# Attention on one Trainium2 core: the last 64 keys scored by one fp32 product in 64x64 tiles at the head of each pair, two GpSimd additions in every pair, and another order of score and maxima units

## Chip, core and metric

One core of one Trainium2 chip runs the kernel. The metric is device time in microseconds (us), the median of repeated runs. Engines are named as the profile names them: PE (TensorE, matrix products), PEld (its weight loads), DVE (VectorE), ACT (ScalarE), POOL (GpSimd), SP (the engine that issues most DMAs).

## What is computed

Attention over 4 batches and 8 heads (576 positions, 64 values per head), then two feed-forward layers on its output. Only the attention changes here:

```python
q_rot, k_rot = (rotate(q), rotate(k))
scores = scale * np.matmul(q_rot, k_rot.transpose(0, 1, 3, 2))
scores = scores - np.max(scores, axis=-1, keepdims=True)
attn = np.exp(scores)
attn = attn / (np.sum(attn, axis=-1, keepdims=True) + 1e-09)
return np.matmul(attn, v).astype(np.float32)
```

Everything is float32 with a tight tolerance. A score product is therefore made of three products of rounded parts (high by high, low by high, high by low, each in the type fp32r), or of one product in full fp32.

## The kernel before

**Pairs.** The work is tiled in 16 pairs of heads (`NPAIR`), one after the other. A pair's two heads lie in partitions 0 to 63 and 64 to 127. The feed-forward layers follow the 16 pairs and are not touched.

**What a pair's phase does.** `phase(i)` interleaves two kinds of unit on PE, each into one of four PSUM slots `PS[0]` to `PS[3]` (two banks each):

- score units of pair i, `st_unit`: letter `t` in the order string, eight per pair, 128 keys by 288 queries. Each has four products for each of the two heads (L663): three of rounded parts, and one that subtracts the row maxima (`one_r` by `mr`). The two heads use the upper and lower half of the array at once (tile form 64x128). ACT then takes the exponential into a tile `E`. Letter `T` is the ninth unit, for the last 64 keys: eight products of the form 128x128 (L671), whose weights `KRH` and `KRL` are block-diagonal copies of the last keys, made by DMAs.
- maxima units of pair i+1, `s_unit`: its own scores in one rounded product, from which DVE takes row maxima. Letter `x` (two per pair) covers two query chunks by 256 keys, `y` (four) one chunk by 320 keys (both L611), `S` the last 64 queries (L621, form 128x128). `s_end` combines the maxima, and three small DMAs lay them out as the row tile `MR` of the next pair.

The order is a string that is written out by hand, `"ytyttxtttyttyxTS"`. `phase` gives each unit a slot by a small model of when slots come free: among the free ones the latest freed, else the one that is free first. The last four units use only slots 0 to 2.

**After the phase**, still in pair i: eight groups of fp32 products of `E` with the values into `PS[3]` (L700, tiles 128x32), the row sums by products with ones (L735, `sum_unit`), and the values of the last 64 keys (L710, tiles 64x64, four at once). ACT and DVE copy `PS[3]` out as `xu`. `add_unit` lets POOL add some `E` tiles beforehand into `AC`, so that the row sums need fewer products: two additions for pairs before `FOUR` (9) and for the last, four for pairs 9 to 14. Two additions leave four groups of four products in `sum_unit`, four additions three.

**Beside it** DVE rotates q and k of pair i+2 in the tile `RAW` (`prep_high`, two buffers), ACT casts the high parts `QP`, `QH`, `KH`; POOL subtracts for the low part `QL`, and for `KL` up to pair 9; from then on `KL` is DVE's. `prep_load` loads `RAW` of pair i+2. In the earlier pairs DVE also converts weights of the next layer (`wa_half`).

**Order.** A planner (`Plan`) lists the tasks of each engine by modelled times; PE's tasks keep the order in which the code adds them.

Of the kernel before, what the change touches and what calls it, by code (L numbers as in the profile page):

```python
# [23 lines left out]
FOUR = 9  # L24
# [146 lines left out]
def mixer_kernel(ctx: ExitStack, tc: tile.TileContext, qk, v, vrem, cs, w_in, g_ln, w_sgT, b_sg,  # L171
# [58 lines left out]
    KRH = tiles(att, "krh", 3, [128, 128], F32R)  # L230
    KRL = tiles(att, "krl", 3, [128, 128], F32R)
    MR = tiles(att, "mr", 2, [128, S], F32R)
    MX = tiles(att, "mx", 2, [128, 2, 2, 4], F32)
    MN = tiles(att, "mn", 2, [128, 10], F32R)
    VM = tiles(att, "vm", 2, [128, 4, 2, 64], F32)
    VR = tiles(att, "vr", 2, [128, 64], F32)
# [8 lines left out]
    one_r = att.tile([128, 128], F32R, name="one_r")  # L245
    one_b = att.tile([128, 128], F32R, name="one_b")
# [29 lines left out]
    def setup():  # L276
        def zeros(k):
            for t in (QR[k], KRH[k], KRL[k]):
                nc.gpsimd.memset(t.bitcast(F32), 0.0)
        def consts():  # L280
            nc.gpsimd.memset(one_r.bitcast(F32), 0.0)
            nc.gpsimd.memset(one_b.bitcast(F32), 0.0)
            for h in range(2):
                nc.gpsimd.memset(ones_b[h], 0.0)
            nc.gpsimd.memset(ones, 1.0)
            nc.gpsimd.memset(mhalf, -0.5)
            for t in (*XS, *RB):
# [163 lines left out]

    def dg(q, dst, src):
        for h in range(2):
            q.dma_start(out=dst[64 * h:64 * h + 64, 64 * h:64 * h + 64].bitcast(F32),
                        in_=src[64 * h:64 * h + 64, 512:576].bitcast(F32))
    def first_pairs():
# [29 lines left out]
        def cast_qp(i, x, y, n):  # L486
            acopy(lambda: QP[i][:, :, x // 4:y // 4], lambda: RAW[i][:, 0, 0, x:y].rearrange("r (p c) -> r c p", c=4), n,
                  [("raw", i, 0, 0), ("raw", i, 0, 1)][x // HALF:1 + (y > HALF)], [("qpx" if y < 512 else "qp", i)])

        def low(i, j, r=()):  # L490
# [3 lines left out]
            if j:  # L494
                dma(32, lambda q: dg(q, KRL[i], KL[i]), [("kl", i)], [("krl", i)], n=2)

        def diagonals(i, j):
            hi, to, kh, kt = ((QH, QR, "qh", "qr"), (KH, KRH, "kh", "krh"))[j]
            dma(32, lambda q: dg(q, to[i], hi[i]), [(kh, i)], [(kt, i)], n=2)
# [14 lines left out]
        cast_qp(0, 0, 512, 1100)  # L514
# [4 lines left out]
        diagonals(0, 0)  # L519
        diagonals(0, 1)  # L520
# [17 lines left out]
        cast_qp(1, 0, 512, 1100)  # L538
# [4 lines left out]
        diagonals(1, 0)  # L543
        diagonals(1, 1)
# [14 lines left out]
    def prep_high(i, after):  # L559

        j2, j3 = i % 2, i % 3
        for j in (0, 1):
            raw, kr = RAW[j2][:, j], ("raw", j2, j)
            tt("D", lambda raw=raw: raw, lambda raw=raw: raw, lambda: cst, ALU.mult, 2 * S, [("cst",)], [kr], after)
            after = [tt("D", lambda raw=raw: raw[:, 0], lambda raw=raw: raw[:, 0], lambda raw=raw: raw[:, 1], ALU.add, S, [], [kr])]
            if j:
                acopy(lambda: KH[j3], lambda raw=raw: raw[:, 0], S, [kr], [("kh", j3)])
                dma(32, lambda q: dg(q, KRH[j3], KH[j3]), [("kh", j3)], [("krh", j3)], n=2)
            else:
                acopy(lambda: QP[j2], lambda raw=raw: raw[:, 0, 0:512].rearrange("r (p c) -> r c p", c=4), 1100, [kr], [("qp", j2)])  # L570
# [4 lines left out]
    def low_part(e, i, j, after):  # L575
# [5 lines left out]
        if j:  # L581
            dma(32, lambda q: dg(q, KRL[j3], KL[j3]), [("kl", j3)], [("krl", j3)], n=2)
# [7 lines left out]
    def load_v(i, after=()):  # L590
        j2 = i % 2

        def ld(q):
            q.dma_start(out=VM[j2].rearrange("p c h d -> p (c h d)"), in_=v[i // HP, i % HP])
            q.dma_start(out=VR[j2], in_=vrem[i // HP, i % HP])
        dma(290, ld, w=[("vm", j2), ("vr", j2)], after=after, n=2)

    def s_unit(i, n, ps, kps):
# [3 lines left out]
        if n < 6:  # L602
# [10 lines left out]
            add("PE", MAXIMA[n // 2 > 0][0], mm, [("qp", j2), ("kh", j3) if i > 1 or n > 1 else ("khx", i), *[("qpx", i)][:i == 0]], [kps])  # L613
# [12 lines left out]
    def s_end(i):  # L626
# [21 lines left out]
    ne = [0]  # L648
    EU = {}

    def st_unit(i, u, ps, kps):
# [3 lines left out]
        if u < 8:  # L655
# [3 lines left out]
            def mm():  # L659
                for o, (x, y) in enumerate(((kh, qh), (kl, qh), (kh, ql), (one_r, mr))):  # L660
                    for h in range(2):
                        rows = slice(64 * h, 64 * h + 64)
                        nc.tensor.matmul(ps[:, h, 0:HALF], x[rows, keys] if o < 3 else x[rows], y[rows, cols],  # L663
                                         start=o == 0, stop=o == 3)
            add("PE", 4 * PASS, mm, [("qh", j3), ("ql", j3), ("kh", j3), ("kl", j3), *[("mr", j2, x) for x in range(2 + hf)], ("consts",)], [kps])
        else:
            def mm():
                for hf in range(2):
                    cols = slice(HALF * hf, HALF * hf + HALF)
                    for o, (x, y) in enumerate(((KRH[j3], qh), (KRL[j3], qh), (KRH[j3], ql), (one_b, mr))):  # L670
                        nc.tensor.matmul(ps[:, hf, 0:HALF], x, y[:, cols], start=o == 0, stop=o == 3)  # L671
            add("PE", 8 * PASS + 0.2, mm, [("krh", j3), ("krl", j3), ("qh", j3), ("ql", j3), *[("mr", j2, x) for x in range(3)], ("consts",)], [kps])
        n = ne[0] % 9
        ne[0] += 1
        EU[i, u] = n
# [14 lines left out]
    def pv_unit(i, us):  # L690
# [15 lines left out]
        def mm():  # L706
            for hf in range(2):
                for h in range(2):
                    rows = slice(64 * h, 64 * h + 64)
                    nc.tensor.matmul(pv[64 * hf:64 * hf + 64, h, 0:HALF], VR[j2][rows], e[rows, hf], start=False, stop=True,  # L710
                                     skip_group_check=True)
        add("PE", FP32 + 0.1, mm, [("e", EU[i, 8]), ("vr", j2)], [kp])
# [4 lines left out]
        def st(q):  # L717
            for hf in range(2):
                q.dma_start(out=xu_d[i // HP][i % HP, :, HALF * hf:HALF * hf + HALF].rearrange("(h d) c -> d h c", h=2),
                            in_=xu[64 * hf:64 * hf + 64])  # L720
        dma(290, st, [("xu", j2, h) for h in range(2)], [("xu_d", i)], n=2)

    def sum_unit(i, ps, kps):

        j2 = i % 2
        src = [(ones, ones, [(E[EU[i, u + hf]], h) for h in range(2) for hf in range(2)], ("e", EU[i, u]),
# [517 lines left out]
```

## Time and profile before

| | |
|---|---|
| median of 3 runs | 552.18 us (551.42 to 552.51) |
| the profiled execution, own time | 550.86 us |
| its span | 549.1 us |
| PE busy | 541.2 us (99%) |
| DVE, ACT, POOL busy | 76%, 51%, 45% |
| granted PE clock | 0.999 of full speed |

The span runs from the first to the last instruction that the profile holds; the execution's own time is 1.8 us longer. Products on PE overlap: a product's row begins when its weights load or its first column goes in, and the time from one row's start to the next tells the pace, not the row's length. The columns of each view are said with its first group below.

### The profile page before, as it was taken

To read this page: it belongs to the slowest core of one execution; us is meant where nothing else is said; L and a number is where in the kernel's file an instruction comes from. 1 tells how busy PE (TensorE), PEld (TensorE's weight loads), DVE (VectorE), ACT (ScalarE), POOL (GpSimd) and SP (SyncE) were. 2 spreads that over 40 slices of the span, in tenths; PEclk is the share of its full clock that TensorE was granted. 3 is DMA by queue.
4 is the path that set the end of the run, shared out by engine and by line. 5 is a ranking of instruction groups with operands and counts; after the bars stand their busy time and mean duration, and the time that the engine had idled before them with its cause. 6 is when DMAs were issued, how large, how long until landed. Compare 5 with 4: busy or idle time off the path is not lost.

```text
span 549.1 us, 12848 instructions
## 1 busy us (share of the span) xinstructions
PE 541.2 (99%) x5104; PEld 462.5 (84%) x5104; DVE 416.6 (76%) x611; ACT 278.4 (51%) x451; POOL 245.7 (45%) x229
## 2 busy tenths in 40 slices
PE   7999999999999999999999999999999999999996
PEld 6877777777777777679989989989999998899985
DVE  7878888888888888878478845663989997659610
ACT  3566767667766667635527136135156443333221
POOL 6545555555555555446886776653610011222000
PEclk9999999999999999999999999999999999999999
DMA  5565656565556673773384752634264212110022
GB/s 193 136 186 154 194 143 189 150 178 175 168 164 161 185 205 95 216 240 93 133 280 134 223 198 74 210 113 144 106 214 130 66 45 78 38 58 1 0 78 96
DMA packets 58028, 77.46 MB, mean 141 GB/s; under 512 B 29392, under 2 KB 34000, under 8 KB 57968
## 3 DMA queue, kind: packets, MB, share of 16 engines
q1 hardware_dynamic: 57664, 76.37, 45.8%
q8 instruction: 40, 0.66, 0.5%
q10 hardware_dynamic: 304, 0.26, 0.1%
q14 instruction: 20, 0.16, 0.1%
HBM read 55.94 MB, written 18.95 MB: 136 GB/s over the span
## 4 chain that ended last, share of the span: by engine, by line
PE 97%; DVE 1%; POOL 0%; ACT 0%; issue 0%; ACTq 0%; POOLq 0%
PE psa L843 55%; PE psa L663 13%; PE psa L700 12%; PE psa L735 5%; PE psa L611 4%; PE psa L671 4%; PE psa L710 2%; PE psa L954 2%; PE psa L756 1%; DVE mx L614 1%; PE psa L621 1%; DVE raw L260 0%; DVE mn L623 0%; POOL mr L295 0%; ACT ob L264 0%
## 5 line engine op out<-in xcount | busy, mean ns | idle before, releaser
L614 DVE TENSOR_REDUCE mx<-psa 128x2 f32<-128x640 f32 (+1 forms) x96 | 88.7, 954 | 21.9 <-PE psa L611 14.6
L676 ACT ACTIVATE e<-psa 128x576 f32<-128x576 f32 x144 | 88.1, 652 | 20.9 <-PE psa L671 10.3
L700 PE MATMUL psa<-e,vm 128*32 128x288 f32 x1024 | 65.4, 408 | 0.0
L700 PEld LDWEIGHTS psa<-e,vm 128*32 128x32 f32 x1024 | 31.6, 110 | 27.8 <-issue 2.6
L261 POOL TENSOR_TENSOR ac<-e,e 128x576 f32<-128x576 f32 x32 | 45.0, 1425 | 8.2 <-ACT e L676 8.2
L843 PE MATMUL psa<-s_h,vn 128*128 128x288 f32 x256 | 46.9, 295 | 0.0
L260 DVE TENSOR_TENSOR raw<-raw,cst 128x1152 f32<-128x1152 f32 (+1 forms) x33 | 41.9, 1271 | 0.3 <-DMA raw<-qk 0.3
L264 ACT CAST qp<-raw 128x512 fp32r<-128x512 f32 x16 | 19.1, 1192 | 43.6 <-DVE raw L260 43.6
L663 PE MATMUL psa<-qh,kh 64*128 64x288 f32 x256 | 39.6, 305 | 0.0
L843 PEld LDWEIGHTS psa<-s_h,vn 128*128 128x128 f32 x256 | 38.3, 188 | 0.0
L663 PE MATMUL psa<-qh,kl 64*128 64x288 f32 x256 | 37.9, 292 | 0.0
L663 PE MATMUL psa<-ql,kh 64*128 64x288 f32 x256 | 37.9, 292 | 0.0
L663 PE MATMUL psa<-mr,one_r 64*128 64x288 f32 x256 | 37.7, 290 | 0.0
L261 POOL TENSOR_TENSOR vs<-vs,u 128x576 f32<-128x576 f32 x16 | 26.7, 1666 | 20.7 <-DVE vs L958 20.7
L611 PE MATMUL psa<-kh,qp 64*128 64x320 f32 (+1 forms) x256 | 32.8, 312 | 0.7 <-ACT kh L264 0.7
L1035 DVE SCALAR_TENSOR_TENSOR gt<-xm,cw,gt 128x576 f32<-128x576 f32 x32 | 28.9, 909 | 1.8 <-ACT gt L1032 1.4
L611 PEld LDWEIGHTS psa<-kh,qp 64*128 64x128 f32 x256 | 21.6, 184 | 8.0 <-ACT ss L739 3.9
L843 PE MATMUL psa<-XL,w_h 128*128 128x288 f32 x128 | 27.4, 296 | 0.0
L843 PE MATMUL psa<-XH,w_h 128*128 128x288 f32 x128 | 27.4, 295 | 0.0
L843 PE MATMUL psa<-XH,w_l 128*128 128x288 f32 x128 | 27.4, 295 | 0.0
L843 PE MATMUL psa<-s_l,vn 128*128 128x288 f32 x128 | 27.2, 294 | 0.0
L261 POOL TENSOR_TENSOR xl<-xs,xh 128x576 fp32r<-128x576 f32 x2 | 4.6, 2322 | 48.8 <-ACT xh L264 48.8
(182 smaller groups left out, 1488.2 us busy)
## 6 DMA issues: line engine op xcount, KB each, us to landing
raw<-qk SPq DMA_DIRECT2D x31, 576.0 KB
xu_d<-xu SPq DMA_DIRECT2D x32, 144.0 KB
rb<-r_d SPq DMA_DIRECT2D x32, 144.0 KB
xs<-xu_d SPq DMA_DIRECT2D x16, 288.0 KB
x_d<-xs SPq DMA_DIRECT2D x16, 288.0 KB
g_d<-vs SPq DMA_DIRECT2D x16, 288.0 KB
vm<-v SPq DMA_DIRECT2D x16, 256.0 KB
wr<-w_in SPq DMA_DIRECT2D x8, 512.0 KB
```

The costliest lines, as they stand in the source:

```text
L260: return add("DVE", dve(n), lambda: nc.vector.tensor_tensor(out_(), a(), b(), op), r, w, after, lock=True)
L261: return add("Pool", pool(n), lambda: nc.gpsimd.tensor_tensor(out_(), a(), b(), op), r, w, after, lock=True)
L264: return add("Act", act(n), lambda: nc.scalar.copy(out_(), in_()), r, w, after)
L611: nc.tensor.matmul(ps[:, h, w * y:w * y + w], QP[j2][rows, c], kh[rows, keys], start=True, stop=True)
L614: add("DVE", MAXIMA[n // 2 > 0][1], lambda: nc.vector.tensor_reduce(out=MX[j2][:, n // 2 > 0, :, chunks[0]:chunks[-1] + 1], in_=ps[:, :, 0 ...
L663: nc.tensor.matmul(ps[:, h, 0:HALF], x[rows, keys] if o < 3 else x[rows], y[rows, cols], start=o == 0, stop=o == 3)
L671: nc.tensor.matmul(ps[:, hf, 0:HALF], x, y[:, cols], start=o == 0, stop=o == 3)
L676: add("Act", 0.62, lambda: nc.scalar.activation(E[n], ps[:, :, 0:HALF], AF.Exp), [kps], [("e", n)])
L700: nc.tensor.matmul(pv[32 * t:32 * t + 32, h, 0:HALF], VM[j2][:, j, h, 32 * (t % 2):32 * (t % 2) + 32], E[EU[i, us[t // 2]]][:, h], start=j ...
L735: nc.tensor.matmul(ps[32 * t:32 * t + 32, 0, 0:HALF], x[t // 2], a[:, y], start=n == 0, stop=n == len(src) - 1, skip_group_check=True)
L843: nc.tensor.matmul(out_(y), lhs(p, k, y), rhs(q, k, y), start=not z, stop=ends and z == len(terms) - 1)
L1035: add("DVE", dve(S) + 0.05, lambda dd=dd, m=m, x2=x2, gt=gt: nc.vector.scalar_tensor_tensor(gt(), x2()[:, m:m + S], cw[:, 5 * dd + m:5 * d ...
```

## The change

- **Last 64 keys.** `t_unit(i)` stands at the head of pair i, right behind the last product of pair i-1: four fp32 products (64 keys by 288 queries; two heads by two query halves) on the rotated `RAW` tile itself, into `PS[0]`. Unit `T` is then only the two products that subtract the maxima. `KRH`, `KRL`, `one_b` and the DMAs that filled them are gone.
- **Maxima row.** `MR` is folded to 288 columns (four rows in place of two), with one `one_r` for each query half. Every score unit now waits for all three of its DMAs.
- **Order.** `T` comes first, `S` into the middle of the phase (or, in pair 0, one unit before the end), an `x` near the end.
- **Additions.** `FOUR` is 15: two POOL additions in all pairs, and `KL` by POOL in all pairs.
- **Smaller things.** k's rotation sum and its cast are cut at column 256 (one more DVE and one more ACT instruction per pair). The values of the last keys come with the others in one DMA, `xu` leaves in one. `RAW` of pair i+2 is loaded behind `t_unit(i)`, since that now reads the same buffer. At the start 29 products of 288 columns keep PE going in place of 16 of 512.

```diff
-FOUR = 9
+FOUR = 15
+FREE3 = 1.2
+ORDERS = 'xtyTtyttyytxttSt', 'TytytxttStyyttxt', 'Ttttttttt'
...
+    def t_unit(i):
+
+        raw = RAW[i % 2]
+
+        def mm():
+            for hf in range(2):
+                for h in range(2):
+                    rows = slice(64 * h, 64 * h + 64)
+                    nc.tensor.matmul(PS[0][64 * hf:64 * hf + 64, h, 0:HALF], raw[rows, 1, 0, 512:S], raw[rows, 0, 0, HALF * hf:HALF * hf + HALF],
+                                     start=True, stop=False, skip_group_check=True)
+        add("PE", FP32 + 0.1, mm, [("raw", i % 2, j) for j in range(2)], [("ps", 0)])
...
         else:
             def mm():
-                for hf in range(2):
-                    cols = slice(HALF * hf, HALF * hf + HALF)
-                    for o, (x, y) in enumerate(((KRH[j3], qh), (KRL[j3], qh), (KRH[j3], ql), (one_b, mr))):
-                        nc.tensor.matmul(ps[:, hf, 0:HALF], x, y[:, cols], start=o == 0, stop=o == 3)
...
+                for h in range(2):
+                    rows = slice(64 * h, 64 * h + 64)
+                    nc.tensor.matmul(ps[:, h, 0:HALF], one_r[2][rows], mr[rows], start=False, stop=True, skip_group_check=True)
...
-            order = "ytyttxtttyttyxTS" if i + 1 < NPAIR else "ttttttttT"
-            if not i:
-                order = "xtttyttytyttyxTS"
-            free = [0.0, 0.0, 0.74 if i else 0.0, 0.0]
-            pe, ac, dv = 0.2, 0.0, 0.0
+            order = ORDERS[1 if i + 1 < NPAIR else 2] if i else ORDERS[0]
+            free = [9.9, 0.0, 0.5 if i else 0.0, FREE3]
+            pe, ac, dv = 0.58, 0.85, 0.0
...
+                k = 0 if what == "T" else max(at_once, key=lambda k: free[k]) if at_once else min(ks, key=lambda k: free[k])
...
         for i in range(NPAIR):
+            t_unit(i)
             if i + 2 < NPAIR:
                 prep_load(i + 2)
```

**Place one, PE at the head of a pair** (`kh`, `qp`: operands of the maxima units; `mr` with `one_r`: the maxima row). Before:

```order
L735 MATMUL psa<-e_166,ones_b_181 32x288 x2
L710 MATMUL psa<-e_166,vr_156 64x288 x4
L611 MATMUL psa<-kh_133,qp_137 128x320 x2
L663 MATMUL psa<-qh_126,kh_132 128x288 x2
L663 MATMUL psa<-qh_126,kl_135 128x288 x2
```

Now:

```order
L717 MATMUL psa<-e_158,vm_149 64x288 x4
L657 MATMUL psa<-raw_123 64x288 x4
L680 MATMUL psa<-mr_142,one_r_171 128x288 x2
L610 MATMUL psa<-kh_131,qp_138 128x320 x2
L673 MATMUL psa<-qh_127,kh_133 128x288 x2
```

Four fp32 products of the form 64x64 and two of the form 64x128 have come in between the last values product and the first maxima unit.

**Place two, PE at the end of a phase before**, where the two units of the form 128x128 stand side by side:

```order
L611 MATMUL psa<-kh_133,qp_137 128x256 x4
L671 MATMUL psa<-qh_126,krh_143 128x288
L671 MATMUL psa<-qh_126,krl_146 128x288
L671 MATMUL psa<-ql_129,krh_143 128x288
L671 MATMUL psa<-mr_149,one_b 128x288
L621 MATMUL psa<-kh_133,qr_141 128x288 x2
L700 MATMUL psa<-e_158,vm_155 32x288 x2
```

And now, where `S` (L620) is the only one left and stands between two score units:

```order
L673 MATMUL psa<-ql_130,kh_133 128x288 x2
L673 MATMUL psa<-mr_142,one_r_170 128x288 x2
L620 MATMUL psa<-kh_131,qr_139 128x288 x2
L673 MATMUL psa<-qh_127,kh_133 128x288 x2
L673 MATMUL psa<-qh_127,kl_136 128x288 x2
```

The eight products of the old ninth unit are gone, and the 128x128 form is entered and left in mid-phase.

## Rows read from the trace of the kernel before

**Rows 1.** The page, part 1: busy us (share of the span) xinstructions.

```profile
PE 541.2 (99%) x5104; PEld 462.5 (84%) x5104; DVE 416.6 (76%) x611; ACT 278.4 (51%) x451; POOL 245.7 (45%) x229
```

**Rows 2.** The page, part 4: the chain that ended last, by engine and line.

```profile
PE 97%; DVE 1%; POOL 0%; ACT 0%; issue 0%; ACTq 0%; POOLq 0%
PE psa L843 55%; PE psa L663 13%; PE psa L700 12%; PE psa L735 5%; PE psa L611 4%; PE psa L671 4%; PE psa L710 2%; PE psa L954 2%; PE psa L756 1%; DVE mx L614 1%; PE psa L621 1%; DVE raw L260 0%; DVE mn L623 0%; POOL mr L295 0%; ACT ob L264 0%
```

**Rows 3.** PE timeline, one pair: start us, us, engine, line, operation, out<-in, tile, xcount.

```profile
101.14 0.41 PE L611 MATMUL psa<-kh,qp 64*128 64x320 f32 x2
101.39 0.29 PE L663 MATMUL psa<-qh,kh 64*128 64x288 f32 x2
...
102.58 0.40 PE L663 MATMUL psa<-qh,kh 64*128 64x288 f32 x2
102.81 0.29 PE L663 MATMUL psa<-qh,kl 64*128 64x288 f32 x2
...
106.32 0.55 PE L611 MATMUL psa<-kh,qp 64*128 64x320 f32 x6
106.80 0.40 PE L671 MATMUL psa<-qh,krh 128*128 128x288 f32 x1
107.03 0.30 PE L671 MATMUL psa<-qh,krl 128*128 128x288 f32 x1
...
107.97 0.42 PE L621 MATMUL psa<-kh,qr 128*128 128x288 f32 x2
108.32 4.09 PE L700 MATMUL psa<-e,vm 128*32 128x288 f32 x64
```

**Rows 4.** PE timeline in the first 20 us: an `S` between 64x128 products.

```profile
11.64 0.69 PE L762 MATMUL psa<-kh,qp 64*128 64x288 f32 x8
12.26 0.53 PE L621 MATMUL psa<-kh,qr 128*128 128x288 f32 x2
12.72 0.79 PE L762 MATMUL psa<-kh,qp 64*128 64x288 f32 x8
```

**Rows 5.** The chain in order of time: start us, us, what; with four and with three sum groups.

```profile
108.39 4.02 PE psa L700 x64
112.40 1.94 PE psa L735 x32
114.34 0.65 PE psa L710 x8
...
193.72 1.46 PE psa L735 x24
```

**Rows 6.** DVE and ACT timelines beside those products (in brackets: idle before, releaser).

```profile
101.71 1.54 DVE L614 TENSOR_REDUCE mx<-psa 128x2 f32<-128x640 f32 x2
108.23 0.65 ACT L676 ACTIVATE e<-psa 128x576 f32<-128x576 f32 x1 [0.42 <-PE psa L671]
223.34 4.45 ACT L676 ACTIVATE e<-psa 128x576 f32<-128x576 f32 x8 [0.40 <-PE psa L663]
```

**Rows 7.** Groups by form: line engine op out<-in forms xcount | busy us, mean ns.

```profile
L614 DVE TENSOR_REDUCE mx<-psa 128x2 f32<-128x640 f32 x64 | 51.1, 821 | 15.1 <-PE psa L611 7.8 <-ACT e L676 7.3
L614 DVE TENSOR_REDUCE mx<-psa 128x4 f32<-128x1024 f32 x32 | 38.9, 1220 | 6.8 <-PE psa L611 6.8
L623 DVE TENSOR_REDUCE mn<-psa 128x1 fp32r<-128x576 f32 x16 | 12.0, 752 | 0.0
```

**Rows 8.** Windows, one pair each: stretch, its us, busy us of PE PEld DVE ACT POOL.

```profile
101.14:114.92 13.78, 13.78 (x199) 10.01 (x195) 12.14 (x20) 9.37 (x15) 7.14 (x6) 1.00 0.42 95
181.00:194.33 13.33, 13.33 (x194) 9.77 (x190) 11.62 (x16) 8.62 (x15) 7.83 (x7) 1.00 0.68 183
```

**Rows 9.** SP and DVE timelines: `RAW` loads issued, and first used.

```profile
97.04 0.95 SPq L556 DMA_DIRECT2D raw<-qk  x2
109.61 1.30 DVE L260 TENSOR_TENSOR raw<-raw,cst 128x1152 f32<-128x1152 f32 x1
```

More of the change, by code (lines that the diff above doesn't have):

```diff
@@ L244, in mixer_kernel @@
     WT.append(att.tile([128, 512], F32, name="wt1"))
-    one_r = att.tile([128, 128], F32R, name="one_r")
-    one_b = att.tile([128, 128], F32R, name="one_b")
+    one_r = [att.tile([128, 128], F32R, name=f"one_r{x}") for x in range(3)]
     ones = att.tile([128, 32], F32, name="ones")
@@ L277, in zeros @@
         def zeros(k):
-            for t in (QR[k], KRH[k], KRL[k]):
-                nc.gpsimd.memset(t.bitcast(F32), 0.0)
+            nc.gpsimd.memset(QR[k].bitcast(F32), 0.0)
         def consts():
-            nc.gpsimd.memset(one_r.bitcast(F32), 0.0)
-            nc.gpsimd.memset(one_b.bitcast(F32), 0.0)
+            for x in range(3):
+                nc.gpsimd.memset(one_r[x].bitcast(F32), 0.0)
             for h in range(2):
@@ L493, in low, with diagonals @@
                [("raw", i, j, 0), ("raw", i, j, 1), (kh, i), *r], [(kl, i)])
[L494 to L499, printed above, removed]
+        def diagonals(i):
+            dma(32, lambda q: dg(q, QR[i], QH[i]), [("qh", i)], [("qr", i)], n=2)
         dma(738, lambda q: [table(q), raw_load(q, 0, 0, slice(0, S))], first=True,
@@ L564, in prep_high @@
             tt("D", lambda raw=raw: raw, lambda raw=raw: raw, lambda: cst, ALU.mult, 2 * S, [("cst",)], [kr], after)
[L565 to L570, printed above, removed]
+            for cc in (slice(0, 256), slice(256, S)) if j else (slice(0, S),):
+                after = [tt("D", lambda raw=raw, cc=cc: raw[:, 0, cc], lambda raw=raw, cc=cc: raw[:, 0, cc], lambda raw=raw, cc=cc: raw[:, 1, cc],
+                            ALU.add, cc.stop - cc.start, [], [kr])]
+                if j:
+                    acopy(lambda cc=cc: KH[j3][:, cc], lambda raw=raw, cc=cc: raw[:, 0, cc], cc.stop - cc.start,
+                          [("khx", j3), kr][0:2] if cc.start else [], [("khx", j3), ("kh", j3)][cc.start > 0:], after)
+            if not j:
+                acopy(lambda: qp4(j2), lambda raw=raw: head(raw[:, 0]), 1100, [kr], [("qp", j2)])
                 acopy(lambda: QH[j3], lambda raw=raw: raw[:, 0], S, [kr], [("qh", j3)])
@@ L591, in load_v @@
         j2 = i % 2
[L593 to L596, printed above, removed]
+        dma(322, lambda q: q.dma_start(out=VM[j2].rearrange("p c h d -> p (c h d)"), in_=v[i // HP, i % HP]), w=[("vm", j2)], after=after)
     def s_unit(i, n, ps, kps):
@@ L708, in mm @@
                 for h in range(2):
-                    rows = slice(64 * h, 64 * h + 64)
-                    nc.tensor.matmul(pv[64 * hf:64 * hf + 64, h, 0:HALF], VR[j2][rows], e[rows, hf], start=False, stop=True,
+                    rows = slice(64 * hf, 64 * hf + 64)
+                    nc.tensor.matmul(pv[64 * h:64 * h + 64, hf, 0:HALF], VM[j2][rows, 4, h], e[rows, h], start=False, stop=True,
                                      skip_group_check=True)
-        add("PE", FP32 + 0.1, mm, [("e", EU[i, 8]), ("vr", j2)], [kp])
+        add("PE", FP32 + 0.1, mm, [("e", EU[i, 8]), ("vm", j2)], [kp])
         xu = XU[j2]
@@ L755, in keep_busy @@
         for _ in range(n):
-            add("PE", 0.24, lambda: nc.tensor.matmul(PS[3][:, 0], one_r, MR[1][:, 0:512], start=True, stop=True),
+            add("PE", PASS, lambda: nc.tensor.matmul(PS[3][:, 0, 0:HALF], one_r[0], MR[1], start=True, stop=True),
                 [("consts",), ("mr", 1, 0), ("mr", 1, 1)], [("ps", 3)])
```

118 lines of the change are left out of this document (59 added, 59 removed).

## The prediction

> **What bounds the kernel now.** I read the page first: PE is busy for 99% of the span [rows 1], and the chain that ended last is PE to 97% [rows 2]. So I ask of the change only what it does to PE's own sequence, and whether another engine or a transfer comes to stand in it. DVE is busy for 12.1 us of one pair's 13.78, POOL for 7.1 [rows 8]: room, but not much on DVE. The feed-forward part (55% of the chain is its line L843) is the same before and after; the end moves with the end of attention. A difference of 0.2% (1.1 us) is about what a measurement of this kernel can tell from none.
>
> In one pair's timeline [rows 3] the prices of PE's steps are starts minus starts:
> - A product of 288 columns: 107.03 to 107.97 holds seven, 0.134 us each. The two heads' products of the form 64x128 run side by side at that price, so a `t` of four is 0.53. `y` is about 0.15, `x` 0.24, `S` 0.26.
> - **A change of tile form costs about 0.2 us.** `y` and `x` take 0.38 of products, but from 106.32 to 106.80 lie 0.48, and the first 128x128 product takes 0.23 in place of 0.13: 0.10 and 0.10. An `S` between 64x128 products shows both directions [rows 4]: from 11.64 to 12.72 lie 1.08 us for four 64x128 products (0.53) and `S` (0.26), and the product behind it takes 0.10 longer (0.79 against 0.69): 0.39 for going in and out. Into `y` behind L710 it is 0.21, from `S` to L700 0.12 (108.32 minus 107.97 is 0.35; two products are 0.26).
> - **A wait for a PSUM slot.** The product at 102.58 takes 0.23 in place of 0.13. The slot of its unit is the first `y`'s, whose DVE maximum began at 101.71 and takes 0.82 [rows 6, 7], to 102.53. So a unit whose slot comes free late starts 0.16 after that: 0.06 to the weight load, 0.10 of load that nothing covers.
>
> **The change, step by step, on PE.**
> 1. The old ninth unit goes: eight products 1.06, and the change of form into it 0.20.
> 2. `t_unit`: four fp32 products in 64x64 tiles, four at once. The same kind stands in L710; fp32 work of four tiles at once costs 4.02 us for 64 records [rows 5], 0.50 for the 8 records here; I take 0.49. It stands right behind L717 (L710's new number) in the same form: no change of form. The two `mr` products behind it: 0.13, and the change to 64x128 that `y` paid before.
> 3. `S` moves to mid-phase: both directions 0.40 where it shared the unit `T`'s entry before; and the phase now ends in a `t`, whose change to L700 I take as 0.16 (bounds 0.12, the row from `S`, and 0.21, the row into `y`).
>
> Products and changes of form, without waits: -1.06 - 0.20 + 0.49 + 0.13 + 0.40 + 0.04 = **-0.20 us a pair**.
>
> 4. **Slot waits.** Here the new order decides, so I walked it: each unit in the slot that `phase`'s rule gives it, with the prices above; ACT starts 0.26 after a unit's last product is handed over (107.97 to 108.23 [rows 3, 6]), holds the slot 0.65, and takes the next 0.55 later at the earliest (eight in 4.45 us [rows 6]); DVE starts 0.26 after and holds the slot 0.82 for `y`, 1.22 for `x`, 0.75 for `S` [rows 7], each 0.09 shorter for its successor (two `y` in 1.54 [rows 6]). Time zero is the end of L710's products (101.03 in rows 3). The old order walked this way reaches L700 at 7.35 (the rows: 7.3) with 0.20 us of waits, the largest 0.11 on the third `t`, where the rows have 0.10. The new order, slots 0 to 3, start times:
>
> T/0 0.69; y/2 0.83; t/1 0.97; y/3 1.50; **t/0 1.90**; x/2 2.43; t/1 2.67; t/3 3.20; S/0 3.93; t/1 4.39; y/2 4.92; y/3 5.07; **t/0 5.37; t/1 5.99**; x/2 6.52; **t/0 6.97**, to 7.50; L700 at 7.66.
>
> The waits: the second `t` could start at 1.65 but gets slot 0 from `T`, whose exponential runs from 1.09 to 1.74: 0.25. The sixth `t` waits for `S`'s maximum (4.45 to 5.21), 0.16; the seventh for the exponential of the fifth, 0.09; the eighth for that of the sixth, 0.21, with only three slots left. Sum 0.71 in place of 0.20. So a phase gets 7.66 - 7.35 = **+0.31 us**: PE does less and waits more. With every delay at the lower or upper end of what the rows show (start after a product 0.20 to 0.29, slot to product 0.10 to 0.20, change of form halved or whole) the difference lies between 0 and +0.35.
>
> The Trainium skill, page "TensorEngine Tiling (Array Packing)", section Performance Considerations (PSUM Bottleneck), says that tiling speeds up TensorE but not the evacuation of PSUM. By PE's work alone a pair would gain 0.20; by that rule the gain goes into waits, and the rows' durations side with it, since ACT and DVE still evacuate the same seventeen units.
>
> 5. **The sums.** Pairs 9 to 14 have four additions now and get two: a fourth group of ones products, 1.94 - 1.46 = 0.48 [rows 5]. They are PE-bound too (13.33 busy of 13.33 [rows 8]), so six times 0.48 = 2.9 us, whole.
> 6. **Ends.** Pair 15 has no maxima units and so few waits: -1.26 + 0.62 by steps 1 and 2, less up to 0.5 if its second `t` waits in slot 3 for a busy DVE: I take -0.4 (-0.6 to 0). Pair 0 has its `T` in mid-phase without a change of form, but walked the same way it waits 0.8 behind `T`: +0.3 (-0.5 to +0.5). The start: 29 times 288 columns are 2% more than 16 times 512, and GpSimd fills more one-row constants before them: +0.2 (0 to 0.4).
>
> **Costed at nothing.** The two cut instructions (about 0.1 us on DVE, 0.2 on ACT): both have room [rows 8]; without it DVE would pass 0.1 a pair on. `KL` by POOL in the late pairs: it loses two additions of the same size there. The `RAW` loads: issued at 97.04, used from 109.61 [rows 9]; now they leave about 0.5 us into the phase, and the rotation begins about 0.6 us behind L700, at 8.3, so 7.8 us are left; if a load came late, each microsecond would show as DVE idle and then as a late `y` of the next pair. The maxima row: all units wait for all three of its DMAs, but `S` is reduced 3 us before the last `x`, and the values products (6.5 us) lie between the last DMA and `T`; a late row would stop PE at `T`. SP has four DMAs fewer for `KRH` and `KRL`, one for `xu` and one for the values.
>
> **The sum.** Pairs 1 to 8: 8 x 0.31 = 2.5. Pairs 9 to 14: 6 x (0.31 + 0.48) = 4.7. Pairs 0 and 15 and the start: +0.1. Together **+7.3 us** on the profiled execution's 550.86: 558.2. The median of the runs lies 1.3 above that execution; against it I predict 552.18 + 7.3 = **559.5 us**.
>
> **The rivals.**
> - *The waits do not come (faster).* If ACT, emptied early by `T`, and DVE free the slots before PE asks, a phase is -0.20 and the old waits of 0.20 go as well: -0.4 for 14 pairs, -5.6, +2.9 for the sums, -0.3 at the ends: 549.2. It decides at about 0.12 us of waits a pair: below that the kernel is faster by over 0.2%. For it: in the old phase PE waited in only one or two places. Against it: the slot times are sums of measured rows, and the walk puts the old waits where they are. Chance 0.13.
> - *A third of the waits (no change).* At 0.12 to 0.26 us of waits a pair the phase gives 0.28 to 0.14 back, in 14 pairs just about the 3.0 of the sums and the ends: 551.1 to 553.3. Chance 0.12.
> - *DVE and POOL become the bound as well (slower).* The planner lets DVE's and POOL's work on SBUF alternate (12.1 us with the maxima, and 7.1, in a pair of 13.78 [rows 8]); if POOL's order, with the split of the next layer's weights now first, pushes the rotation back by 0.3 us a pair, pairs 1 to 8 add 2.4: 562. For it: DVE's load is the highest after PE. Against it: the pair itself gets longer, to 14.1. Chance 0.10.
> - *The load or the row comes late* (above): 1 us in 14 pairs, 573. Chance 0.03.
> - *The change does not do what it says*: the order shows the products removed and added; nothing left to chance.
>
> **How the numbers follow.** The forecast (phase -0.1 to +0.4) has 0.62; with the two slower rivals 0.75 for slower by over 0.2%, 0.12 for the same, 0.13 for faster. The range runs from 551.0, which leaves out most of the faster case, through the same and the walk's lower bound (phase 0, ends -1: 554), to 562.5 (phase +0.4, ends +1.2, or the third rival). The forecast's own range is 553.5 to 562.
>
> **What the profile will show.** Pairs 1 to 8 some 14.1 us apart, pairs 9 to 14 the same 14.1 (before 13.8 and 13.3). In a phase: 0.23 in place of 0.13 at the second, sixth and eighth `t`, and around `S`; no wait at `T`. Idle of DVE larger than now. I am wrong if pairs come closer than 13.7 us, if L657 takes more than 0.5, or if PE waits for `raw` or `mr`.

## The result, and the profile after

| | before | after |
|---|---|---|
| median of 4 runs each | 551.8 us (551.1 to 552.51) | 557.7 us (557.55 to 558.52) |
| ratio, 95% interval | | 1.011 (1.0092 to 1.0128) |
| the profiled execution, own time | 550.86 us | 557.63 us |
| its span | 549.1 us | 555.8 us |

The change makes the kernel slower by 1.1%: 5.9 us between the medians, 6.7 between the two profiled spans (7.3 were predicted). The page of the changed kernel, part 1 and part 4, beside [rows 1, 2]:

```profile
PE 546.7 (98%) x5197; PEld 455.3 (82%) x5197; DVE 423.8 (76%) x619; ACT 283.4 (51%) x465; POOL 237.2 (43%) x217
...
PE 96%; DVE 2%; DMA 1%; ACT 0%; issue 0%; SPq 0%; DVEq 0%; ACTq 0%
PE psa L853 54%; PE psa L673 15%; PE psa L707 12%; PE psa L738 6%; PE psa L610 3%; PE psa L717 2%; PE psa L964 2%; PE psa L657 1%; DVE raw L258 1%; PE psa L620 1%; DVE mx L613 1%; PE psa L680 1%; DMA raw<-qk 1%; DVE mn L622 0%; ACT e L683 0%
```

PE is still nearly the whole chain. Score units (L673) have grown from 13 to 15% of it with as many products in them as before (1024): the growth is waits and the change of form behind `S`, which the chain books on the product that is held up. Sums (L738) have grown from 5 to 6%.

The chain in order of time shows the pace of the pairs as the distance from one L707 to the next, early and late, and the sums (start us, us, what; beside [rows 5]):

```profile
96.68 4.02 PE psa L707 x64
...
110.74 4.02 PE psa L707 x64
...
181.04 4.02 PE psa L707 x64
185.06 1.94 PE psa L738 x32
...
195.10 4.02 PE psa L707 x64
```

All pairs from 1 to 14 stand 14.06 us apart (14.04 to 14.08). In the kernel before it was 13.79 up to pair 9 and 13.32 behind it (one pair of each kind in [rows 8]); there the late sums took 1.46 us [rows 5], here 1.94. So a phase costs 0.27 more, and the fourth group of sums 0.47 more in each of the six pairs 9 to 14.

Where the 0.27 lies is seen in one pair's PE timeline (beside [rows 3]; from one row's start to the next is the pace):

```profile
103.10 0.67 PE L657 MATMUL psa<-raw 64*64 64x288 f32 x8
103.69 0.40 PE L680 MATMUL psa<-mr,one_r 64*128 64x288 f32 x2
103.93 0.31 PE L610 MATMUL psa<-kh,qp 64*128 64x320 f32 x2
...
104.61 0.31 PE L610 MATMUL psa<-kh,qp 64*128 64x320 f32 x2
104.93 0.40 PE L673 MATMUL psa<-qh,kh 64*128 64x288 f32 x2
105.17 0.30 PE L673 MATMUL psa<-qh,kl 64*128 64x288 f32 x2
...
106.73 0.29 PE L673 MATMUL psa<-mr,one_r 64*128 64x288 f32 x2
106.95 0.53 PE L620 MATMUL psa<-kh,qr 128*128 128x288 f32 x2
107.41 0.40 PE L673 MATMUL psa<-qh,kh 64*128 64x288 f32 x2
107.65 0.30 PE L673 MATMUL psa<-qh,kl 64*128 64x288 f32 x2
...
108.04 0.46 PE L610 MATMUL psa<-kh,qp 64*128 64x320 f32 x4
108.40 0.40 PE L673 MATMUL psa<-qh,kh 64*128 64x288 f32 x2
108.64 0.29 PE L673 MATMUL psa<-qh,kl 64*128 64x288 f32 x2
...
109.03 0.38 PE L673 MATMUL psa<-qh,kh 64*128 64x288 f32 x2
109.25 0.30 PE L673 MATMUL psa<-qh,kl 64*128 64x288 f32 x2
...
109.64 0.40 PE L610 MATMUL psa<-kh,qp 64*128 64x256 f32 x4
...
110.18 0.29 PE L673 MATMUL psa<-qh,kl 64*128 64x288 f32 x2
...
110.45 0.29 PE L673 MATMUL psa<-mr,one_r 64*128 64x288 f32 x2
110.67 4.09 PE L707 MATMUL psa<-e,vm 128*32 128x288 f32 x64
```

From the start of a `y` to the end of the first product behind it should pass 0.15 + 0.13 = 0.28; 104.61 to 105.17 is 0.56: the second `t` waits 0.28. Read the same way, the sixth waits 0.17 (108.04 to 108.64), the seventh 0.09 (109.03 to 109.25), the eighth 0.17 (109.64 to 110.18): 0.71 us together. `S` with the last product ahead of it and the first behind it takes 0.92 (106.73 to 107.65) where these products are worth 0.52: 0.40 for the two changes of form. The rows of ACT and DVE name whom the waits are for, here those of the second and the sixth `t`:

```profile
104.22 1.30 ACT L683 ACTIVATE e<-psa 128x576 f32<-128x576 f32 x2 [0.51 <-PE psa L680]
```

```profile
107.59 0.76 DVE L622 TENSOR_REDUCE mn<-psa 128x1 fp32r<-128x576 f32 x1 [0.35 <-PE psa L620]
```

The first of the two exponentials is `T`'s; it starts at 104.22 and holds the slot 0.65, to 104.87, and the second `t`'s product stands at 104.93. `S`'s maximum ends at 108.35, the sixth `t` stands at 108.40.

### The profile page after: what moved, and what is told of

Read it like the earlier page. It is cut to its first block, busy times and chain, and to the rows that moved or that the text cites. A ratio compares the mean times of both kernels' runs of the same rounds, so it can differ in the third digit from the quotient of the medians.

```text
span 555.8 us, 12881 instructions
## 1 busy us (share of the span) xinstructions
PE 546.7 (98%) x5197; PEld 455.3 (82%) x5197; DVE 423.8 (76%) x619; ACT 283.4 (51%) x465; POOL 237.2 (43%) x217
## 4 chain that ended last, share of the span: by engine, by line
PE 96%; DVE 2%; DMA 1%; ACT 0%; issue 0%; SPq 0%; DVEq 0%; ACTq 0%
PE psa L853 54%; PE psa L673 15%; PE psa L707 12%; PE psa L738 6%; PE psa L610 3%; PE psa L717 2%; PE psa L964 2%; PE psa L657 1%; DVE raw L258 1%; PE psa L620 1%; DVE mx L613 1%; PE psa L680 1%; DMA raw<-qk 1%; DVE mn L622 0%; ACT e L683 0%
## 5 line engine op out<-in xcount | busy, mean ns | idle before, releaser
L683 ACT ACTIVATE e<-psa 128x576 f32<-128x576 f32 x144 | 91.1, 652 | 29.6 <-PE psa L673 17.2
L707 PE MATMUL psa<-e,vm 128*32 128x288 f32 x1024 | 65.4, 408 | 0.0
L707 PEld LDWEIGHTS psa<-e,vm 128*32 128x32 f32 x1024 | 31.6, 110 | 27.8 <-issue 2.4
L673 PE MATMUL psa<-qh,kh 64*128 64x288 f32 x256 | 45.5, 352 | 0.5 <-ACT e L683 0.4
L673 PE MATMUL psa<-qh,kl 64*128 64x288 f32 x256 | 37.7, 292 | 0.0
L673 PE MATMUL psa<-ql,kh 64*128 64x288 f32 x256 | 37.7, 291 | 0.0
L673 PE MATMUL psa<-mr,one_r 64*128 64x288 f32 x256 | 37.5, 290 | 0.0
L673 PEld LDWEIGHTS psa<-qh,kh 64*128 64x128 f32 x256 | 23.9, 184 | 11.4 <-ACT e L683 6.7
L610 PE MATMUL psa<-kh,qp 64*128 64x320 f32 (+1 forms) x256 | 30.4, 294 | 0.6 <-ACT kh L262 0.6
L258 DVE TENSOR_TENSOR raw<-raw 128x576 f32<-128x576 f32 (+3 forms) x48 | 30.0, 647 | 1.1
L259 POOL TENSOR_TENSOR ql<-raw,qh 128x576 fp32r<-128x576 f32 x16 | 24.0, 1500 | 13.8 <-ACT qh L262 13.8
```

Source lines behind the costliest of these rows:

```text
L258: return add("DVE", dve(n), lambda: nc.vector.tensor_tensor(out_(), a(), b(), op), r, w, after, lock=True)
L259: return add("Pool", pool(n), lambda: nc.gpsimd.tensor_tensor(out_(), a(), b(), op), r, w, after, lock=True)
L610: nc.tensor.matmul(ps[:, h, w * y:w * y + w], QP[j2][rows, c], kh[rows, keys], start=True, stop=True)
L683: add("Act", 0.62, lambda: nc.scalar.activation(E[n], ps[:, :, 0:HALF], AF.Exp), [kps], [("e", n)])
L707: nc.tensor.matmul(pv[32 * t:32 * t + 32, hf, 0:HALF], VM[j2][:, j, t // 2, 32 * (t % 2):32 * (t % 2) + 32], E[EU[i, us[hf]]][:, t // 2], ...
```

## The experiments

Distances between pairs are L707 to L707, as above; a pair's distance is that from the pair ahead of it to itself, and the column "pairs 10 to 14" leaves out pair 9, where the sums ahead are still of the early kind. Medians of before in the three sets of runs: 551.31 us for e1 to e4, 551.58 for f1 to f4, 552.03 for g1 to g3.

| run | median us | ratio to before (95%) | pairs 1 to 8 | pairs 10 to 14 |
|---|---|---|---|---|
| e1: FOUR = 9 | 555.7 | 1.0056 to 1.0092 | 14.05 | 13.62 |
| e2: low-wait order | 556.09 | 1.0061 to 1.0110 | 13.4 to 15.8 | 13.45 |
| e3: order of before behind T | 564.66 | 1.0222 to 1.0252 | 14.03, one 17.59 (pair 9: 17.88) | 14.03 |
| e4: half exponentials | 551.41 | 0.9980 to 1.0014 | 13.60 | 13.6, one 13.75 |
| f1: order with two waits | 554.48 | 1.0033 to 1.0075 | 13.81 | 13.82 |
| f2: two orders, FOUR = 9 | 551.7 | 0.9974 to 1.0012 | 13.82 | 13.26 to 13.40 |
| f3: before with FOUR = 15 | 553.82 | 1.0030 to 1.0054 | 13.79 | 13.81 |
| f4: head products twice | 565.04 | 1.0221 to 1.0272 | 14.54 | 14.54 |
| g3: first maxima row by SP | 557.78 | 1.0062 to 1.0115 | 14.06 | 14.06 |
| g1: f2, other late order | 550.29 | 0.9943 to 0.9977 | 13.81 | 13.1, one 13.41 |
| g2: g1, other early order | 550.08 | 0.9939 to 0.9973 | 13.77, one 14.09 | 13.07 |

**Are the waits the cause? Shorter holds (e4) and another order (f1).** From pair 1 on, the kernel of e4 leaves out half of the columns of each exponential.

```diff
-        add("Act", 0.62, lambda: nc.scalar.activation(E[n], ps[:, :, 0:HALF], AF.Exp), [kps], [("e", n)])
+        w = HALF // 2 if i else HALF
+        add("Act", 0.62, lambda: nc.scalar.activation(E[n][:, :, 0:w], ps[:, :, 0:w], AF.Exp), [kps], [("e", n)])
```

> The changed kernel with its order; from pair 1 on the exponentials cover only the first 144 of 288 columns (the rest of E keeps pair 0's values), so ACT holds a slot 0.41 us in place of 0.65. PE's instructions are the same. Theory (slot waits): the waits at the second, seventh and eighth t shrink from 0.25, 0.10 and 0.21 to about 0.06 in all, the one behind S's maximum stays at 0.15; L707 0.46 us earlier, 14 x 0.46 = 6.4 us off, 557.7 to 551.3. Rival (PE's own work and changes of form set the phase): no change, 557 to 558. Rival (DVE's maxima set the phase): less than 2 us off.

Measured: 551.41 us, and the pairs 13.60 apart, 0.46 less, with every PE instruction in its old place. In the PE timeline of that run the second `t` follows its `y` 0.14 us later, the pace of a `y`, and the wait behind `S`'s maximum, which was not shortened, is still there (0.36 from the two `y` to the `t`, as in the changed kernel):

```profile
102.42 0.31 PE L610 MATMUL psa<-kh,qp 64*128 64x320 f32 x2
102.56 0.33 PE L673 MATMUL psa<-qh,kh 64*128 64x288 f32 x2
...
105.63 0.46 PE L610 MATMUL psa<-kh,qp 64*128 64x320 f32 x4
105.99 0.40 PE L673 MATMUL psa<-qh,kh 64*128 64x288 f32 x2
```

So the time of a phase is set by when slots come free: a quarter of a microsecond less per exponential on ACT gives more than the whole loss of the phase (0.27) back. By PE's own work nothing would have moved. This run agrees with the rule of the Trainium skill that the prediction weighed (page "TensorEngine Tiling (Array Packing)", section Performance Considerations, PSUM Bottleneck): what the change saved on PE was kept back by the evacuation.

```diff
-ORDERS = 'xtyTtyttyytxttSt', 'TytytxttStyyttxt', 'Ttttttttt'
+ORDERS = 'xtyTtyttyytxttSt', 'TytytytxtStyttxt', 'Ttttttttt'
```

> Only the order of pairs 1 to 14 is changed, T ytytytxt S tyttxt: T, S and the last x stand where the changed kernel has them, one t trades places with a y and the slots come out otherwise. Theory (slot waits): two waits are left, 0.25 behind T's exponential and 0.16 at the last t, 0.41 in place of 0.71; 0.30 us less in each of 14 phases, pairs 13.76 us apart in place of 14.06, 557.7 - 4.2 = 553.5, or 2.0 over the kernel before; DVE's maxima end no later than now, so that the late diagonal of the run with the low-wait order should not come. Rival (work and changes of form, which are the same): pairs stay 14.06 apart, 557 to 558. Rival (any order that lets PE go faster meets DVE): some pairs of 14 us and more, waits at S or at the first y.

Measured: 554.48 us, where 553.5 was expected, and pairs 13.81 apart: 0.24 gained of 0.30 expected, in every pair the same.

```profile
95.52 4.02 PE psa L707 x64
...
109.33 4.02 PE psa L707 x64
```

Two waits are left, as expected: 0.28 at the second `t` (103.45 to 104.01 from its `y`) and 0.16 at another. But that one is the fourth `t`, behind the first `x` (105.09 to 105.62), and not the last, which does not wait (108.41 to 108.78): here the walk had the sum right and one place wrong.

The form of the new score of the last keys is the same here; only letters have traded places. With it a phase is as long as before the change (13.79).

**What a phase without waits would meet (e2, e3).**

```diff
-ORDERS = 'xtyTtyttyytxttSt', 'TytytxttStyyttxt', 'Ttttttttt'
+ORDERS = 'xtyTtyttyytxttSt', 'TyttyttxtStyttxy', 'Ttttttttt'
```

> One string: the order of the units of pairs 1 to 14 is T yttyttxt S tyttxy. T still at the head, S still in mid-phase, so PE's work and changes of form are the same as in the changed kernel. Theory (the phase is longer by its waits for PSUM slots, 0.71 us in the changed kernel): walked by the prediction's prices this order waits 0.03 us and reaches L707 0.68 us earlier, so 14 x 0.68 = 9.5 us off, 557.7 to 548.2, pairs 13.38 us apart. Rival one (the phase is longer by work or changes of form): no change, 557 to 558. Rival two (DVE, with 12.1 us of work in a pair and its maxima now 1.1 us later against L707, becomes the bound): waits of PE at the first y of the next pair, 551 to 555.

Measured: 556.09 us; the second rival, and only in some pairs. Pairs 1 and 2 and those from 10 to 14 are 13.40 to 13.49 apart, near the 13.38 of the walk. From pair 3 to 9, where DVE also converts weights, the distances are 14.62, 13.86, 15.82, 13.85, 14.42, 13.86, 14.61. The chain in time of the longest of them, and PE's row at its end:

```profile
84.95 1.91 DVE raw L258
...
88.77 0.67 ACT qh L262
91.02 4.53 DMA qr<-qh
```

```profile
95.69 0.51 PE L620 MATMUL psa<-kh,qr 128*128 128x288 f32 x2 [1.68 <-DMA qr<-qh]
```

The maxima end later against L707, so the rotation behind them begins later: 2.2 us behind L707 (84.86 against 82.63) in place of 0.8 (111.43 against 110.67). Its first multiplication also takes 1.98 us in place of 1.35, while a subtraction of POOL runs from 84.20 to 85.63. The diagonal `QR` leaves SP behind the first part of the next `RAW` load and lands at 95.55, 4.5 us on, and `S` waits 1.68 us for it. What PE saves in slot waits it then pays as a late operand. The cover that the prediction named for the rotation (DVE has room) is gone in these pairs, whose phases the order would make 0.65 shorter.

```diff
-ORDERS = 'xtyTtyttyytxttSt', 'TytytxttStyyttxt', 'Ttttttttt'
+ORDERS = 'xtyTtyttyytxttSt', 'TytyttxtttyttyxS', 'Ttttttttt'
```

> One string: behind T the order of before, ytyttxtttyttyx, and S last. Theory: S at the end saves 0.24 us a phase of changes of form, but S must wait 0.5 us for its slot and the second t 0.25 behind T, waits 0.81 in all; L707 0.14 us earlier than in the changed kernel, 14 x 0.14 = 2 us off: 555.7. Rival (the waits do not count, the place of S does): 14 x 0.24 = 3.4 us off and more, 554 or less, with no gap at S.

Measured: 564.66 us. Most pairs stand at 14.03, so `S` at the end gains 0.03 and not 0.14. It waits at its slot as the theory had it (0.42 us idle before the row of L620); but the change of form into L707 that its place saves was worth 0.09 in the changed kernel and not the 0.16 of the theory, which is 0.07 of the missing 0.11. The rest of the loss was expected by neither side: two pairs, 5 and 9, take 17.59 and 17.88. DVE's and POOL's timelines, in a pair that is not late and in front of the first late one:

```profile
73.88 0.49 DVE L258 TENSOR_TENSOR raw<-raw 128x320 f32<-128x320 f32 x1
...
89.18 0.46 DVE L722 COPY xu<-psa 128x288 f32<-128x288 f32 x1 [0.88 <-PE psa L717]
89.56 1.85 DVE L258 TENSOR_TENSOR raw<-raw 128x320 f32<-128x320 f32 x1
```

```profile
89.67 1.39 POOL L259 TENSOR_TENSOR kl<-raw,kh 128x576 fp32r<-128x576 f32 x1
```

The second part of k's rotation sum, an addition that takes 0.49 elsewhere in this run, takes 1.85 here: it ends at 91.41, 0.35 behind the end of POOL's subtraction. The cast of k follows, and PE's first `y` waits 2.05 us for it. The addition was also late before it began: in this pair the copy of `xu` stands ahead of it on DVE, and DVE is idle for 0.88 us until PE's L717 releases that copy; in the pair with 0.49 the copy stands behind the addition (at 75.10). So of the 2.05 us some 0.7 (an estimate: 2.05 less 1.36) come from DVE's order and the rest from the long addition. Pair 9 shows the same two things (0.89 idle, 1.84 for the addition). The Trainium skill, page "SBUF — State Buffer", section "SBUF: two separate sides", says that DVE and GpSimd share a pair of ports that one of them holds for a whole instruction while the other blocks. The rows agree: the addition's extra 1.36 us is about POOL's 1.39. Which of the two began first they cannot tell: the addition's row starts 0.11 ahead of POOL's, but while the copy's (to 89.64) still runs. In e2 above POOL was first, and the multiplication was 0.63 longer where 0.77 of the subtraction were left.

**The sums (e1, f3).**

```diff
-FOUR = 15
+FOUR = 9
```

> FOUR back to 9, nothing else. Theory (every addition less on GpSimd is a fourth group of ones products on PE, and PE is the bound in pairs 9 to 14 too): the rise of pairs 9 to 14 that the traces show beyond that of pairs 1 to 8, 0.47 us each, goes: 6 x 0.47 = 2.8 us off the changed kernel, 557.7 to 554.9; pairs 9 to 14 are 13.6 us apart instead of 14.06, pairs 1 to 8 stay at 14.06. Rival (with the additions back, GpSimd or the low part of k back on DVE stands in the way of the new phase): 556 or more, and the late pairs stay above 13.8.

Measured: 555.7 us; early pairs 14.05, late pairs 13.62: 0.44 less in each, for 0.47 expected. The median lies 0.8 over the expected 554.9; in the profiled execution 0.56 of that is the start (its first L707 stands at 26.98, that of the changed kernel at 26.42).

In the kernel before the same constant was set the other way (`-FOUR = 9`, `+FOUR = 15`):

> The kernel before with FOUR = 15 alone: two additions by GpSimd and a fourth group of ones products in all pairs, the low part of k by GpSimd in all pairs. Theory: 0.47 us more in each of six pairs, 2.8 us, 551.6 to 554.4, all pairs 13.8 apart. Rival (the sums are partly hidden in the late pairs, and the slow late pairs of the changed kernel come from its order): less than 1.5 us.

Measured: 553.82 us, 2.2 over before where 2.8 was expected (the interval allows 1.7 to 3.0); its late pairs went from 13.32 to 13.81, 0.49 each, and its early ones did not move. The two runs price the same step from both sides; nothing of the sums is hidden. The constant moves `KL` between DVE and POOL as well, so it is the whole step that is priced, and the ones products alone account for it (0.48).

**The products at the head (f4).** The line that adds `t_unit`'s products to PE stands there twice.

> The changed kernel, where every pair does the four fp32 products at its head twice into the same slot (the same result). Theory (PE is the bound at the head, nothing there is hidden): 0.49 us more in each of 15 pairs; in pair 0 the products stand in front of a wait for the cast of k and cost nothing: 7.4 us on top of 557.7, 565.1, pairs 14.55 apart. Rival (part of it takes the place of a wait, the second t's or T's): 0.25 us a pair or less, 561 or less.

Measured: 565.04 us, pairs 14.54 apart, 0.48 more each. They cost what PE's rows say, whole; no wait behind them gives anything back.

**The start (g3).** Both DMAs that write the halves of the first maxima row are issued by SP; before and in the changed kernel ACT issues one of them.

> The changed kernel, where the first maxima row of the whole kernel is written by two DMAs of SP; ACT issues none. In the changed kernel's trace ACT's own DMA there takes 1.32 us (0.56 before), the casts of q and k of pair 1 stand behind it, and the first maxima unit of pair 0 waits for them: 18.87 in place of 18.24. Theory (that is what pair 0's delay beyond the prediction is): from the end of the keep-busy products at the start to the first maxima unit of pair 0 it is 9.1 us as before, not 9.7, and 0.6 us go over the whole run, less than these rounds can tell: 556.5 to 557.5. Rival (the second DMA on SP lands too late): the first t of pair 0 waits, nothing is won or some is lost. Rival (the delay is DVE's): the maxima unit starts where it did.

Measured: 557.78 us, no difference that can be told. The traces tell it. The changed kernel, PE and ACT:

```profile
3.55 5.67 PE L759 MATMUL psa<-mr,one_r 128*128 128x288 f32 x29 [3.55 <-POOL mr L294]
9.15 0.50 PE L610 MATMUL psa<-kh,qp 64*128 64x256 f32 x4
...
18.87 0.50 PE L610 MATMUL psa<-kh,qp 64*128 64x256 f32 x4 [0.55 <-ACT kh L262]
```

```profile
15.93 1.32 ACTq L635 DMA_DIRECT2D mr<-mn  x1
17.34 1.15 ACT L262 CAST qp<-raw 128x512 fp32r<-128x512 f32 x1 [7.11 <-DMA mr<-mn]
```

And g3's PE:

```profile
3.55 6.83 PE L755 MATMUL psa<-mr,one_r 128*128 128x288 f32 x29 [3.55 <-POOL mr L294]
10.31 0.50 PE L610 MATMUL psa<-kh,qp 64*128 64x256 f32 x4
...
19.35 0.50 PE L610 MATMUL psa<-kh,qp 64*128 64x256 f32 x4
```

From the end of the keep-busy products (the first row of L610) to the first maxima unit of pair 0 (the last row) it is 9.72 us in the changed kernel and 9.04 in g3 (before: 9.05). ACT's issue was the 0.7 us. That g3's profiled execution is no faster all the same comes from its keep-busy products, 6.83 in place of 5.67 us.

**A version that beats both (f2, g1, g2).** f2 gives pairs 9 to 14 the low-wait order, since no weights are converted there, and their four additions:

```diff
-FOUR = 15
+FOUR = 9
-ORDERS = 'xtyTtyttyytxttSt', 'TytytxttStyyttxt', 'Ttttttttt'
+ORDERS = 'xtyTtyttyytxttSt', 'TytytytxtStyttxt', 'TyttyttxtStyttxy', 'Ttttttttt'
...
-            order = ORDERS[1 if i + 1 < NPAIR else 2] if i else ORDERS[0]
+            order = ORDERS[1 + (i >= FOUR) if i + 1 < NPAIR else 3] if i else ORDERS[0]
```

> Three things together: the order above for pairs 1 to 8, the low-wait order T yttyttxt S tyttxy for pairs 9 to 14, where no weights are converted by DVE, and four additions by GpSimd in pairs 9 to 14 again. Theory: pairs 1 to 8 13.76 apart, pairs 9 to 14 at 14.06 - 0.63 (measured with the low-wait order) - 0.44 (measured with the additions) = 13.0; 8 x 0.30 + 6 x 1.07 = 8.8 us off the changed kernel, 548.9, some 2.7 below the kernel before. Rival (GpSimd's two more additions and DVE cannot follow at 13.0): late pairs at 13.3 to 13.6, 551 to 553.

Measured: 551.7 us, where 548.9 was expected, and no difference from before. Early pairs stand at 13.82 (13.76 expected); the late ones are 13.3, not 13.0. PE's timeline shows the first `y` 0.24 late in them (0.48 from L680 in place of 0.24), and ACT's timeline the cast of k just ahead of it, behind the copy of the sums (183.46):

```profile
184.09 0.40 PE L680 MATMUL psa<-mr,one_r 64*128 64x288 f32 x2
184.57 0.41 PE L610 MATMUL psa<-kh,qp 64*128 64x320 f32 x2
```

```profile
183.76 0.75 ACT L262 CAST kh<-raw 128x256 fp32r<-128x256 f32 x2
```

So g1 takes a late order whose maxima end earlier (`TyttyttyttyxtxtS`) and g3's start; g2 also an early order with S at the end (`TytxtytytxtttytS`).

> The combination of before (order T ytytytxt S tyttxt in pairs 1 to 8, four additions by GpSimd in pairs 9 to 14), with another order in pairs 9 to 14, T yttyttyttyxtxt S, whose maxima end 0.4 us earlier against L707, and with the maxima row of pair 0 by SP. Theory: in the combination of before the first y of the late pairs stood 0.24 us behind the cast of k, at the end of the chain maxima, rotation, cast; with 0.4 us more room it does not wait, and its own slot waits are 0.30: late pairs at 14.06 - 0.65 - 0.44 = 13.0 in place of 13.28, 551.7 - 1.7 - 0.6 = 549.4, 0.4% below the kernel before. Rival (DVE and GpSimd together are the limit at 13.28, not that chain): late pairs at 13.2 or more, 551.

> As the run with another late order, and in pairs 1 to 8 T ytxtytytxttty t S without the gap: S last, its form left only towards L707, at the price of slot waits of 0.56. Theory (both count, by their prices): 7.28 in place of 7.36 by the walk, pairs 1 to 8 at 13.73 in place of 13.81, 0.6 us less than that run: 548.8. Rival (an order with S last meets the late cast of k or the diagonal in the pairs in which DVE converts weights): some early pairs of 14 us or more, 551 to 556.

Measured: 550.29 and 550.08 us, 0.9 and 1.3 over what was expected. Late pairs are 13.07 to 13.11 apart (one of g1's 13.41), so it was the chain from the maxima to the cast, not a limit of DVE and GpSimd together. g2's early pairs are 13.76 to 13.79, 0.04 less than g1's, with one of 14.09; that small step can't be told between the medians. g2's chain, two late pairs:

```profile
188.93 4.02 PE psa L703 x64
...
202.01 4.02 PE psa L703 x64
```

Ratio to before 0.9956 (0.9939 to 0.9973): with another order and the sums put right, the kernel with the product at its head is 0.4% faster than the kernel before. That the product is what gains is not shown: the kernel before was not tried with another order. By the prediction's walk it has 0.20 us of waits a pair to lose, which would put its late pairs at 13.1 (an estimate, 13.32 less 0.20), as near as can be told to the 13.07 here.

## Why the prediction was right, step by step

- **What bounds.** Right: PE is 96% of the chain, and doubling 0.49 us of its work (f4) came out at the end as 0.48 a pair.
- **Steps 1 to 3, products and changes of form.** Right: L657 to L680 0.59 (0.49 and the first half of a change of form), no change of form behind L717 (102.56 to 103.10 for L717's eight records, the pace it had before), S 0.40. The last change, into L707, took 0.09 (110.45 to 110.67, less a product) where 0.16 was taken and 0.12 was the lower bound: mis-sized by 0.07. The rows of before had the right size: 108.32 minus 107.97, less two products of 0.13, is 0.09 and not 0.12, so this change costs the same before and after.
- **Step 4, slot waits.** Right in number, place and size: second, sixth, seventh and eighth `t`, 0.28, 0.17, 0.09, 0.17 for 0.25, 0.16, 0.09, 0.21; 0.71 for 0.71. The walk's start times fall within 0.15 us of the rows, and e4 and f1 moved the phase about as the walk says (0.46 for 0.46 and 0.24 for 0.30). The phase is 0.27 longer for 0.31 forecast; the change into L707, 0.07 too large, more than covers the difference. The count of seventeen units that ACT and DVE evacuate is off by one (the order has sixteen letters); nothing hangs on it.
- **Step 5, the sums.** Right: 6 x 0.47 for 6 x 0.48.
- **Step 6, the ends.** The step that failed, by its sizes. Pair 15 gained 0.63 and not 0.4: its L707 stands 11.74 behind pair 14's in place of 11.90, although 0.47 more of sums lie between. That is the prediction's -1.26 + 0.62 whole; the wait of the second `t` that it held against it did not come (its start stands at the pace of the products). The start and pair 0 together cost 0.79 and not 0.5, and for another reason: the prediction priced the keep-busy columns and GpSimd's constants and waits behind `T`, but gave no price to the DMA of the maxima row on ACT's queue. It took 1.32 us there for 0.56 before, the casts of pair 1 stood behind it, and the first maxima unit came at 18.87 for 18.24; pair 0's phase itself grew by 0.16 (18.87 to 26.35, before 18.24 to 25.56).
- **The sum.** 14 x 0.27 + 6 x 0.47 - 0.63 + 0.79 = 6.8 us by these rounded terms, 6.7 between the spans, 7.3 forecast; between the medians 5.9. The predicted median of 559.5 stands 1.8 over the measured one, well inside the range. The two profiled executions differ by more than the medians do because that of before, 550.86, lies 0.9 under its median and that of after at its own. That the ends came so near is in part luck: the start was put at +0.2 and came out at -0.04 (the keep-busy products end at 9.15 us, before at 9.19), but those products differ by up to 1.4 us between the traces of this kernel's family (last section).
- **Costed at nothing.** Right for this order: PE waits for neither `raw` nor `mr`. The expectation that DVE would idle more was wrong: 12.57 us busy of 14.06 (before 12.14 of 13.78), so 1.49 idle for 1.64 before. e2 shows how thin that cover is.
- **The rivals.** "The waits do not come" asked for phases 0.4 shorter than before. e4 took waits away by force and came to 0.19 (13.60 for 13.79), with the wait behind `S`'s maximum still there; e2's undisturbed pairs, with hardly a wait by the walk, came to 0.36 (13.45 for the 13.81 of f3). "DVE and POOL become the bound" did not come with this order, but it did with others: with faster phases in e2, and in two pairs of e3.

## What to carry to other kernels

Where units of two kinds share a few PSUM slots, the order of the units is a term of its own: walk it with the rows' durations, slot by slot, before and after, and count waits of 0.1 to 0.3 us as carefully as products. Work taken off PE is only a gain if the engines that empty the slots keep up, and when the phase does get shorter, the next thing late is the longest chain from one phase's last result to the next one's first operand. Count what is issued on every queue at the start too: a DMA on ACT's queue is time in which ACT casts nothing.

## What the runs showed of the hardware that was not expected

- **PE's clock after a wait.** In e3 PE stood still from 89.9 to 91.95. Windows of that run (stretch, us, busy us of PE, PEld, DVE, ACT, POOL, then the granted clock):

```profile
90.00:92.00 2.00, 0.05 (x2) 0.05 (x2) 1.93 (x4) 1.11 (x2) 1.05 (x1) 1.00 0.55 137
92.00:94.00 2.00, 2.00 (x18) 2.00 (x20) 1.71 (x4) 0.45 (x1) 1.01 (x2) 0.52 0.91 283
94.00:96.00 2.00, 2.00 (x24) 2.00 (x24) 0.71 (x2) 1.12 (x3) 1.03 (x2) 0.62 0.84 269
96.00:98.00 2.00, 2.00 (x32) 1.97 (x32) 1.48 (x2) 1.94 (x4) 1.76 (x2) 1.00 0.97 355
```

  In the 2 us behind the wait the granted clock was 0.52, about the lower of its two levels (1.2 GHz), and products stood 0.24 apart in place of 0.13; from 95.70 on they stood 0.13 apart again, and the window from 96 shows the full clock. The pair lost 3.56 us against its neighbours, 2.05 by the wait and the other 1.5 mostly by the clock.
- **The keep-busy products at the start** took 5.67 us in the changed kernel and 6.83 in g3, the same 29 products of 288 columns; in the other runs of that kernel's family between 5.41 and 6.60. Pair 0 starts later by as much, up to 1.4 us or 0.25% of the kernel's time, which can hide or feign a small change. The rows show where the time goes: the products stand 0.24 apart at first, the pace of e3's slow stretch, up to 6.84 us in the changed kernel and up to 9.47 in g3, and then 0.13. The later step is the whole difference. The granted clock of the window from 2.7 to 10 us reads 1.00 in both all the same; why the step comes when it does is left open.
- **A DMA's issue on ACT** took 1.32 us where SP issued its own 0.06 earlier, and 0.56 in the kernel before, where SP's came 0.30 later. The DMA of SP, which writes the other half of the same folded row, took 0.54, so the folded row alone does not make an issue long on SP; whether the row or the coincidence does it on ACT was not tried.
